# A gated linear attention and a maxout FFN: one masked product of q*P and k/P per chunk in place of seven levels, behind a guard

## The chip, the cores and the metric

One Trainium2 chip, one of its cores. The metric is the device time of one execution in microseconds; shorter is better.

## What is computed

First a linear attention with a decaying state, for 4 batches and 8 heads, 768 tokens, head width 48:

```python
f = 1 / (1 + exp(-f_logit))
for t in range(768):
    state = f[t][:, None] * state + outer(k[t], v[t])   # 48 x 48 per batch and head
    y[t] = q[t] @ state
```

So y_t is the sum over s <= t of v_s times the sum over d of q_t[d] k_s[d] P_t[d] / P_s[d], where P is the running product of the gates. Then an FFN on x, which is y as 3072 tokens of width 384:

```python
h = maximum(maximum(x @ w1, x @ w2), x @ w3)    # 384 -> 768
out = h @ w_out                                  # 768 -> 384
```

The attention's inputs are float32. The four weights come as float64 and are rounded to float32 on the chip. Every matrix product is in float32. The gates are the sigmoid of numbers around 2 (deviation 0.5).

## The kernel before

The tokens are taken in chunks of 128: 24 chunks, batch by batch (`b, c = divmod(u, NCH)`), six of a batch one after the other. Two heads share the 128 partitions, 64 rows each, of which 48 are used; `par` is which of the two, `hp` which of the four pairs of heads.

`chunk(u)` (lines 162 to 253) transposes f, k and q (lines 166 to 172). Then it splits the pairs (s, t) of the chunk into seven levels m = 1, 2, 4 .. 64 (line 186): at a level s lies in the first and t in the second half of an aligned block of 2m tokens. Each level is eight products of 48 x 128 by 48 x 64 (line 192), whose masked parts are copied into `at` (line 197 by VectorE, line 205 by ScalarE), and then the halves of `qh` and `kh` are multiplied by their neighbour's gate product (line 211 VectorE, line 212 GpSimd), on which the next level's products depend. After the levels: the output of the chunk (line 219), the share of the state (line 223), the new state (lines 228 to 242), the pairs s = t (lines 178 to 182, added at line 248), and three transposes that bring the result into `xT`, features on partitions (line 251).

Four chunks make a group, on which `ffn` (line 256) works in 22 steps: 18 with three products of 512 columns (line 263), and four that write 128 tokens (line 274). The weights are rounded by `round_weight` (lines 137 to 152) in 15 pieces, on VectorE, ScalarE and GpSimd, in the first group.

A chunk yields ten times (lines 183, 215, 245, 253), and at each yield the loop of line 298 issues one step of what is pending: the rounding first, then the FFN of the group before. A group has 40 yields for 22 steps. The order on each engine follows this program order closely; a planner moves single instructions ahead where their inputs are ready.

All DMAs are issued by SyncE: four loads a chunk, three chunks ahead, the weights, one store per 128 tokens. An fp32 product is two TensorE instructions, a transpose one.

Of the kernel before, what the change touches and what calls it, by code (L numbers as in the profile page):

```python
# [8 lines left out]
FP32 = mybir.dt.float32  # L9
U32 = mybir.dt.uint32  # L10
AF = mybir.ActivationFunctionType
ALU = mybir.AluOpType
AX = mybir.AxisListType

# y_t = sum_{s<=t} sum_d q_t[d] k_s[d] (prod_{s<u<=t} f_u[d]) v_s, in chunks of C tokens.
#
# Within a chunk the pairs (s, t) are split by levels m = 1, 2, 4 .. C/2: a pair belongs to the
# level whose aligned block of 2m tokens has s in its first half and t in its second. There
#     prod_{s<u<=t} f_u = (product after s to the end of the first half)
#                       * (product from the start of the second half to t),  # L20
# so with KH = k * (products to the end of its block of m) and QH = q * (products from the start of
# its block of m) the level is one matrix product, of which a mask takes the pairs in one block.
# From m to 2m the second halves of QH and the first halves of KH take the product of the whole
# neighbouring block. Every factor is at most 1 and nothing is divided, whatever the gates are.
# After the last level QH and KH are those of the whole chunk: for the state and from the state.
# The pairs s = t are added apart, with the dot product of q_t and k_t.
# [3 lines left out]
def kernel(  # L30
# [14 lines left out]
    C = 128  # L45
    DP = 64  # a head's rows when two heads share the 128 partitions
# [7 lines left out]
    GRP = 4  # chunks in one pass of the FFN  # L54
    TOK = GRP * C
    LEVELS = [1, 2, 4, 8, 16, 32, 64]
    AHEAD = 3

    const = ctx.enter_context(tc.tile_pool(name="const", bufs=1))
    work = ctx.enter_context(tc.tile_pool(name="work", bufs=2))  # L60
    ps_tr = ctx.enter_context(tc.tile_pool(name="ps_tr", bufs=2, space=bass.MemoryType.PSUM))
    ps_a = ctx.enter_context(tc.tile_pool(name="ps_a", bufs=3, space=bass.MemoryType.PSUM))
    ps_y = ctx.enter_context(tc.tile_pool(name="ps_y", bufs=1, space=bass.MemoryType.PSUM))
    ps_f = ctx.enter_context(tc.tile_pool(name="ps_f", bufs=2, space=bass.MemoryType.PSUM))

# [1 line left out]
    ident = const.tile([128, 128], FP32, name="ident")  # L67
    make_identity(nc, ident)

    # level m: key s (partition) against the m * n queries of the second halves (free)  # L70
    masks = {}
    for m in LEVELS[:-2]:
        n = C // (2 * m)
        t = const.tile([C, C // 2], FP32, name=f"mask{m}")
        nc.gpsimd.memset(t, 1.0)
        nc.gpsimd.affine_select(out=t, in_=t, compare_op=ALU.is_ge, fill=0.0, base=0,
                                pattern=[[-2 * m, n], [0, m]], channel_multiplier=1)
        nc.gpsimd.affine_select(out=t, in_=t, compare_op=ALU.is_ge, fill=0.0, base=m - 1,
                                pattern=[[2 * m, n], [0, m]], channel_multiplier=-1)
        masks[m] = t  # L80

    def zeroed(name, n, shape, part):
        ts = []
        for i in range(n):
            t = const.tile(shape, FP32, name=f"{name}{i}")
            nc.vector.memset(part(t), 0.0)
            ts.append(t)
        return ts

    NLD = AHEAD + 1  # L90
    pads = {nm: zeroed(f"{nm}_ld", NLD, [C, H, DP], lambda t: t[:, :, D:DP]) for nm in "qkf"}
    at_tiles = zeroed("at", 2, [C, 2, HP, C], lambda t: t)
    st_tiles = zeroed("st", 2, [128, HP, 2 * D], lambda t: t)
# [5 lines left out]
    loaded = {}  # L99

    def load(u):
        b, c = divmod(u, NCH)
        d = {}
        for nm, src in (("f", f_logit), ("k", k), ("q", q), ("v", v)):
            x = src[b, :, c * C:(c + 1) * C, :].rearrange("h t d -> t h d")
            if nm == "v":
                d[nm] = work.tile([C, H, D], FP32, name="v_ld", bufs=NLD)
                nc.sync.dma_start(out=d[nm], in_=x)
            else:
                d[nm] = pads[nm][u % NLD]  # L110
                nc.sync.dma_start(out=d[nm][:, :, 0:D], in_=x)
        loaded[u] = d

    # Weights come as float32 or as the words of float64, which are rounded to float32 here.
    pieces = [(w_in[i][:, c, :], src[c * 128:(c + 1) * 128, :])
              for i, src in enumerate((moe_w1, moe_w2, moe_w3)) for c in range(NK)]
    pieces += [(w_out[:, j, :], moe_w_out[j * 128:(j + 1) * 128, :]) for j in range(NJ)]
    raw = {}

    def load_weight(n):  # L120
        dst, src = pieces[n]
        if src.dtype == FP32:
            nc.sync.dma_start(out=dst, in_=src)
        else:
            raw[n] = work.tile([128, 2 * DFF], U32, name="raw", bufs=3)
            nc.sync.dma_start(out=raw[n][:, 0:2 * src.shape[1]], in_=src.bitcast(U32))

    def round_weight(n):
        if n not in raw:
            return  # L130
        dst, N = pieces[n][0], pieces[n][1].shape[1]
        words = raw.pop(n)[:, 0:2 * N].rearrange("p (n two) -> p n two", two=2)
        lo, hi = words[:, :, 0], words[:, :, 1]
        # The sign, the exponent and 23 bits of the mantissa. In float32's range the top bit of the
        # exponent and its low seven are float32's exponent.
        top = work.tile([128, N], U32, name="top_bits")
        nc.vector.tensor_scalar(top, hi, 3, 0x3FFFFFF8, op0=ALU.logical_shift_left, op1=ALU.bitwise_and)
        nc.vector.scalar_tensor_tensor(top, hi, 0xC0000000, top, op0=ALU.bitwise_and, op1=ALU.bitwise_or)
        nc.vector.scalar_tensor_tensor(top, lo, 29, top, op0=ALU.logical_shift_right, op1=ALU.bitwise_or)
        # The other 29 bits, times the power of two of the whole: a float32 sum rounds them in.  # L140
        rest = work.tile([128, N], U32, name="rest_bits")
        nc.vector.tensor_scalar(rest, lo, 0x1FFFFFFF, None, op0=ALU.bitwise_and)
        val = work.tile([128, N], FP32, name="rest_val")
        nc.scalar.activation(val, rest, AF.Copy, scale=2.0 ** -52)
        power = work.tile([128, N], U32, name="power")
        nc.vector.tensor_scalar(power, top, 0xFF800000, None, op0=ALU.bitwise_and)
        nc.gpsimd.tensor_tensor(val, val, power.bitcast(FP32), op=ALU.mult)
        nc.gpsimd.tensor_tensor(val, val, top.bitcast(FP32), op=ALU.add)
        # Below float32's normal range: 0.
        expo = work.tile([128, N], U32, name="expo")  # L150
        nc.vector.tensor_scalar(expo, hi, 20, 0x7FF, op0=ALU.logical_shift_right, op1=ALU.bitwise_and)
        nc.vector.scalar_tensor_tensor(dst, expo, 897.0, val, op0=ALU.is_ge, op1=ALU.mult)

# [1 line left out]
    def transposed(x):  # L155
        t = ps_tr.tile([128, HP, C], FP32, name="tr")
        flat = x.rearrange("t h d -> t (h d)")
        for hp in range(HP):
            nc.tensor.transpose(t[:, hp, :], flat[:, hp * 128:(hp + 1) * 128], ident)
        return t  # L160

    def chunk(u, xT):
        c, ld, slot = u % NCH, loaded.pop(u), u % GRP
        at, st, st_new = at_tiles[u % 2], st_tiles[u % 2], st_tiles[(u + 1) % 2]

        tr_f = transposed(ld["f"])
        gate = work.tile([128, HP * C], FP32, name="gate")
        nc.scalar.activation(gate, tr_f.rearrange("p a t -> p (a t)"), AF.Sigmoid)  # L168
        tr_k = transposed(ld["k"])
        kh = work.tile([128, HP, C], FP32, name="kh")  # L170
        nc.scalar.copy(kh, tr_k)
        tr_q = transposed(ld["q"])
        qh = work.tile([128, HP, C], FP32, name="qh")
        nc.vector.tensor_tensor(qh.rearrange("p a t -> p (a t)"), tr_q.rearrange("p a t -> p (a t)"),
                                gate, op=ALU.mult)

        qk = work.tile([C, H, D], FP32, name="qk")
        nc.gpsimd.tensor_tensor(qk, ld["q"][:, :, 0:D], ld["k"][:, :, 0:D], op=ALU.mult)
        dot = work.tile([C, H], FP32, name="dot")
# [156 lines left out]
```

## Time and profile before

| | us |
|---|---|
| three runs | 1162.44, 1164.34, 1164.58 (median 1164.34) |
| the profiled execution, first to last instruction | 1161.0 |
| the median of the runs above that span | 3.3 |
| TensorE busy | 957.2 |
| VectorE busy | 455.5 |
| mean granted TensorE clock | 0.828 |

A granted clock of 1.00 is 2.4 GHz, 0.50 is 1.2 GHz. Matmuls are pipelined: their durations overlap, so their rate is read from the distance between starts. PE is TensorE, PEld its weight loads, DVE VectorE, ACT ScalarE, POOL GpSimd, SP SyncE; a q behind the name is the engine's queue.

### The profile page before, as it was taken

How to read it: one execution, taken by the hardware profiler on the slowest of the kernel's cores; microseconds unless marked ns; L12 is line 12 of the kernel's file. 1: busy time of each engine (PE TensorE's matmuls, PEld its weight loads, DVE VectorE, ACT ScalarE, POOL GpSimd, SP SyncE). 2: the span in 40 equal slices, each digit the busy share in tenths (PEclk: the TensorE clock that was granted, in tenths of full speed). 3: DMA queues.
4: the chain of work that ended last, by engine and by line, in shares of the span. 5: the costliest groups of instructions: out<-in, count | busy, mean ns of one | idle time of the engine just before them, and what ended most of it. 6: DMA issues, size and time to landing. Idle time of an engine off the chain costs nothing. (4 is left out here: it accounts for less than half of the span.)

```text
span 1161.0 us, 12337 instructions
## 1 busy us (share of the span) xinstructions
PE 957.2 (82%) x4768; PEld 699.2 (60%) x4768; DVE 455.5 (39%) x913; ACT 135.5 (12%) x312; POOL 224.3 (19%) x267
## 2 busy tenths in 40 slices
PE   5501577799997799988799987799977899977898
PEld 4401567666566766667756667756666756666644
DVE  4899832343323243332244333244233234233110
ACT  0111011011111011111011101101111111100000
POOL 4455511211211111111211111111111111111000
PEclk9999985589995589985599985599975599965599
DMA  9233110011021011021011021011011000000000
GB/s 196 75 109 72 31 28 15 14 28 28 1 55 28 1 28 28 1 55 28 7 21 28 8 48 28 9 20 28 15 42 28 7 1 1 14 14 1 1 1 27
DMA packets 105514, 33.83 MB, mean 29 GB/s; under 512 B 100464, under 2 KB 103536, under 8 KB 105456
## 3 DMA queue, kind: packets, MB, share of 16 engines
q1 hardware_dynamic: 105456, 33.04, 13.6%
q8 instruction: 38, 0.62, 0.2%
q14 instruction: 20, 0.16, 0.0%
HBM read 28.31 MB, written 4.72 MB: 28 GB/s over the span
## 5 line engine op out<-in xcount | busy, mean ns | idle before, releaser
L192 PE MATMUL a<-qh,kh 48*128 48x64 f32 x2688 | 368.0, 345 | 119.1 <-DVE qh L211 87.7
L192 PEld LDWEIGHTS a<-qh,kh 48*128 48x128 f32 x2688 | 342.9, 251 | 192.3 <-POOL kh L212 102.3
L263 PE MATMUL p<-xT,w_in 128*128 128x512 f32 x648 | 307.8, 612 | 0.6 <-ACT xT L252 0.6
L197 DVE COPY_PREDICATED at<-mask,a 128x256 f32<-128x256 uint32 x240 | 126.3, 555 | 192.3 <-PE a L192 190.0
L212 POOL TENSOR_TENSOR kh<-kh,tot 128x256 f32<-128x256 f32 x144 | 103.4, 718 | 470.1 <-PE a L192 362.2
L263 PEld LDWEIGHTS p<-xT,w_in 128*128 128x128 f32 x648 | 116.4, 193 | 111.8 <-issue 106.1
L211 DVE TENSOR_TENSOR qh<-qh,tot 128x256 f32<-128x256 f32 x144 | 84.1, 584 | 127.9 <-PE a L192 127.9
L274 PE MATMUL p<-w_out,hm 128*128 128x384 f32 x288 | 98.3, 488 | 0.0
L205 ACT COPY at<-a 32x128 f32<-32x128 f32 x144 | 42.0, 292 | 384.9 <-PE a L192 381.2
L219 PEld LDWEIGHTS y<-v_ld,at 128*128 128x128 f32 x384 | 70.5, 274 | 6.5 <-issue 4.8
L274 PEld LDWEIGHTS p<-w_out,hm 128*128 128x128 f32 x288 | 52.5, 190 | 31.3 <-issue 0.5
L219 PE MATMUL y<-v_ld,at 128*128 128x48 f32 x384 | 71.0, 351 | 0.0
L212 POOL TENSOR_TENSOR kh<-kh,gate 128x256 f32<-128x256 f32 x24 | 20.3, 845 | 239.1 <-PE a L192 239.1
L251 PE MATMUL tr<-ident,x 128*128 128x128 f32 x72 | 16.9, 361 | 59.3 <-DVE x L248 59.3
L269 DVE TENSOR_TENSOR top<-p,top 128x512 f32<-128x512 f32 x36 | 24.9, 692 | 83.9 <-PE p L263 83.8
L251 PEld LDWEIGHTS tr<-ident,x 128*128 128x128 f32 x72 | 12.6, 199 | 64.2 <-issue 61.7
L267 ACT COPY top<-p 128x512 f32<-128x512 f32 x36 | 21.1, 585 | 254.3 <-PE p L263 254.3
L269 DVE TENSOR_TENSOR hm<-p,top 128x512 f32<-128x512 f32 x36 | 24.9, 691 | 61.3 <-PE p L263 61.3
L248 DVE TENSOR_TENSOR x<-y,own 128x384 f32<-128x384 f32 x24 | 13.4, 557 | 87.5 <-PE y L223 78.7
L182 POOL TENSOR_TENSOR own<-v_ld,dot 128x384 f32<-128x384 f32 x24 | 20.1, 837 | 111.7 <-DVE x L248 110.8
L214 DVE TENSOR_TENSOR tot<-gate 128x256 f32<-128x256 f32 x24 | 10.2, 425 | 74.9 <-ACT gate L168 74.9
L233 PE MATMUL tr<-v_ld,ks 128*128 128x96 f32 x160 | 33.0, 372 | 7.5 <-ACT ks L230 7.5
(50 smaller groups left out, 585.0 us busy)
## 6 DMA issues: line engine op xcount, KB each, us to landing
raw<-in_moe_w_dram SPq DMA_DIRECT2D x9, 768.0 KB, 4.4
f_ld<-in_f_logit_dram SPq DMA_DIRECT2D x24, 192.0 KB, 3.2
k_ld<-in_k_dram SPq DMA_DIRECT2D x24, 192.0 KB, 4.0
q_ld<-in_q_dram SPq DMA_DIRECT2D x24, 192.0 KB, 3.8
v_ld<-in_v_dram SPq DMA_DIRECT2D x24, 192.0 KB, 2.6
out_dram<-o SPq DMA_DIRECT2D x24, 192.0 KB, 1.9
raw<-in_moe_w_out_dram SPq DMA_DIRECT2D x6, 384.0 KB, 3.1
```

The source lines that it names most:

```text
L192: nc.tensor.matmul(a[:, hp, :].rearrange("s (n m) -> s n m", m=m), lhsT=kh[r, hp, :], rhs=qh[r, hp, :].rearrange("p (n two m) -> p n two m ...
L197: nc.vector.copy_predicated(at[:, par].rearrange("s a (n two m) -> s a n two m", two=2, m=m)[:, :, :, 1, :], masks[m].bitcast(U32).rearran ...
L205: nc.scalar.copy(at[s0:s0 + m, par, :, s0 + m:s0 + 2 * m], a[s0:s0 + m, :, i * m:(i + 1) * m])
L211: nc.vector.tensor_tensor(qv, qv, tv[:, :, 0:1].to_broadcast([128, nb, m]), op=ALU.mult)
L212: nc.gpsimd.tensor_tensor(kv, kv, tv[:, :, 1:2].to_broadcast([128, nb, m]), op=ALU.mult)
L219: nc.tensor.matmul(y[:, h * D:(h + 1) * D], lhsT=at[:, h % 2, h // 2, :], rhs=ld["v"][:, h, :], start=(h == 0), stop=(c == 0 and h == H - ...
L233: nc.tensor.matmul(ds[:, hp, :], lhsT=ks[:, hp, :], rhs=ld["v"][:, 2 * hp:2 * hp + 2, :].rearrange("s h d -> s (h d)"), start=True, stop=True)
L251: nc.tensor.transpose(tr_x[:, i, :], x[:, i * 128:(i + 1) * 128], ident)
L263: nc.tensor.matmul(p, lhsT=w_in[i][:, kt, j * 128:(j + 1) * 128], rhs=xT[:, kt, :], start=(kt == 0), stop=(kt == NK - 1))
L267: nc.scalar.copy(top, p)
L269: nc.vector.tensor_tensor(hm[:, j, :] if i == 2 else top, p, top, op=ALU.max)
L274: nc.tensor.matmul(p[:, 0:DM], lhsT=hm[:, j, i * C:(i + 1) * C], rhs=w_out[:, j, :], start=(j == 0), stop=(j == NJ - 1))
```

## The change

The kernel becomes two functions and a branch. `fast()` does all the work by another scheme. `general()`, the scheme of before (with its chunk and FFN one after the other), stands behind `tc.If(n_low > 0)`, where `n_low` counts the partitions in which one of the chunks' gate products fell below 2^-64.

In `fast()`:

- P, the running product of the gates inside a chunk, comes from a scan on VectorE, with a floor of 2^-80; 1/P from a reciprocal. `kh = k/P`, `qh = q*P` on GpSimd. The pairs of a chunk are then one product per head (eight of 48 x 128 by 48 x 128) and one mask, s <= t included. The levels, the products s = t and their addition are gone.
- The output is computed transposed, features on partitions (64 columns of weights per head), and ten DMAs per chunk pack its rows (48 of 64) into `xT`. The three transposes of before are gone.
- The chunks go round the four batches (`c, b = divmod(u, B)`), with a state per batch; a group of the FFN is one chunk of each batch.
- `gates(u + 1)` is issued ahead of `pairs(u)`. Five steps of the pending FFN or rounding are issued per chunk at three places, and what is left of them after the group's last chunk.
- The weights come in 12 pieces of 768 columns.

```diff
+            def gates(u):
+                f_ld, k_ld, q_ld = (pads[nm][u % NLD] for nm in "fkq")
+                tr_f = transposed(f_ld)
+                ...
+                nc.scalar.activation(gate, tr_f, AF.Sigmoid)
+                for hp in range(HP):
+                    nc.vector.tensor_tensor_scan(prod[:, hp, :], gate[:, hp, :], floor, 1.0,
+                                                 op0=ALU.mult, op1=ALU.max)
+                for hp in range(HP):
+                    nc.vector.reciprocal(inv[:, hp, :], prod[:, hp, :])
+                ... (transposes of k and q, ScalarE copies kt and qt)
+                nc.gpsimd.tensor_tensor(kh, kt, inv, op=ALU.mult)
+                nc.gpsimd.tensor_tensor(qh, qt, prod, op=ALU.mult)
+                nc.gpsimd.tensor_copy(ends[:, u, :], prod[:, :, C - 1])
+            def pairs(u):
+                ...
+                for hp in range(HP):
+                    for par in range(2):
+                        r = slice(par * DP, par * DP + D)
+                        nc.tensor.matmul(a[:, par, hp, :], lhsT=kh[r, hp, :], rhs=qh[r, hp, :],
+                                         start=True, stop=True)
+                for par in range(2):
+                    nc.vector.tensor_tensor(at[:, par], a[:, par],
+                                            mask.unsqueeze(1).to_broadcast([C, HP, C]), op=ALU.mult)
+                if c < NCH - 1:
+                    ... (kh transposed into tr_s, ScalarE copy ks)
+            def outputs(u, xT):
+                ...
+                for hp in range(HP):
+                    for par in range(2):
+                        nc.tensor.matmul(y[par * DP:(par + 1) * DP, hp, :], lhsT=v_ld[:, 2 * hp + par, :],
+                                         rhs=at[:, par, hp, :], ...)
+                if c < NCH - 1:
+                    ... (ds: the same loops, lhsT=ks[:, 2 * hp + par, :], rhs=v_ld[:, 2 * hp + par, 0:D])
+                if c:
+                    ... (the same loops into y, lhsT=st[r, hp, :], rhs=qh[r, hp, :])
+                nc.scalar.copy(yT, y)
+                if c < NCH - 1:
+                    ... (state: st_new = (ds + st) * tot, VectorE)
+                for h in range(H):
+                    ...
+                        nc.sync.dma_start(out=xT[row % 128:row % 128 + n, row // 128, b * C:(b + 1) * C],
+                                          in_=yT[p0:p0 + n, h // 2, :])
+            gates(0)
+            for u in range(NU):
+                if u + AHEAD < NU:          # AHEAD = 2
+                    load(u + AHEAD)
+                ...
+                if u + 1 < NU:
+                    gates(u + 1)
+                fill(2)
+                pairs(u)
+                fill(1)
+                outputs(u, xT)
+                fill(2)
+                if u % GRP == GRP - 1:
+                    for _ in pending:
+                        pass
+                    pending = ffn(u // GRP, xT)
+            for _ in pending:
+                pass
+            ... (least = min over ends, < 2^-64 as 0 or 1; n_low = their sum by one matmul; low <- n_low)
+    fast()
+    n_low = nc.values_load(low[0:1, 0:1], min_val=0, max_val=128)
+    with tc.If(n_low > 0):
+        general()
```

## Rows read from the trace of the kernel before

**Rows 1.** The page: busy us, share of the span, instructions.
```profile
PE 957.2 (82%) x4768; PEld 699.2 (60%) x4768; DVE 455.5 (39%) x913; ACT 135.5 (12%) x312; POOL 224.3 (19%) x267
```
**Rows 2.** Windows by stage: stretch, length, busy per engine (instructions), clock, DMA share, GB/s.
```profile
core 0: us, PE busy (x) PEld busy (x) DVE busy (x) ACT busy (x) POOL busy (x), PEclk, DMA share, GB/s
0.00:240.00 240.00, 123.31 (x644) 112.77 (x644) 149.44 (x247) 27.00 (x55) 88.81 (x93) 0.85 0.30 65
241.74:344.14 102.40, 101.10 (x520) 62.73 (x520) 38.98 (x84) 13.26 (x31) 16.90 (x21) 1.00 0.15 30
344.14:412.41 68.27, 52.79 (x276) 48.07 (x274) 21.26 (x49) 8.00 (x20) 11.43 (x15) 0.53 0.09 17
...
1092.60:1160.96 68.36, 65.01 (x156) 30.64 (x156) 8.29 (x12) 5.42 (x10) 0.00 (x0) 0.95 0.03 12
```
**Rows 3.** The FFN's products (line 263): ns min/median/max, first and last start.
```profile
L263 PE MATMUL p<-xT,w_in x648: 592/592/1220, 241.9 to 1141.5; 128*128 128x512 f32 x162
```
**Rows 4.** Order of time, TensorE near 30 us: start, us, instruction [idle before, releaser].
```profile
30.24 2.85 PE L192 MATMUL a<-qh,kh 48*128 48x64 f32 x16 [1.20 <-DVE qh L211]
```
**Rows 5.** Order of time, TensorE, in the first stretch at clock 1.00.
```profile
270.80 1.60 PE L192 MATMUL a<-qh,kh 48*128 48x64 f32 x16
272.33 2.84 PE L263 MATMUL p<-xT,w_in 128*128 128x512 f32 x6
275.01 1.88 PE L219 MATMUL y<-v_ld,at 128*128 128x48 f32 x16
276.73 1.10 PE L223 MATMUL y<-st,qh 128*128 128x96 f32 x8
277.66 0.60 PE L228 MATMUL tr<-ident,kh 128*128 128x128 f32 x4
```
**Rows 6.** Windows, line 192 alone, in the sixteen products at 270.80.
```profile
270.80:271.29 0.49, 0.49 (x4) 0.49 (x5) 1.00 0.00 0
271.30:271.69 0.40, 0.40 (x10) 0.40 (x9) 1.00 0.00 0
```
**Rows 7.** Groups by line and shape: count, busy us, mean ns, idle before, releasers.
```profile
L269 DVE TENSOR_TENSOR top<-p,top 128x512 f32<-128x512 f32 x36 | 24.9, 692 | 83.9 <-PE p L263 83.8
...
L230 ACT COPY ks<-tr 128x512 f32<-128x512 f32 x20 | 11.7, 585 | 111.4 <-PE tr L228 111.4
...
L242 DVE TENSOR_TENSOR st<-st,tr 64x192 f32<-64x192 f32 x32 | 11.3, 352 | 19.0 <-PE tr L233 18.7
...
L214 DVE TENSOR_TENSOR tot<-tot 128x128 f32<-128x128 f32 x24 | 7.8, 326 | 0.9
...
L214 DVE TENSOR_TENSOR tot<-tot 128x4 f32<-128x4 f32 x24 | 4.6, 190 | 0.5
```
**Rows 8.** Order of time while the weights are rounded (one period of four).
```profile
58.41 1.98 POOL L147 TENSOR_TENSOR rest_val<-rest_val,power 128x768 f32<-128x768 f32 x1 [3.63 <-DVE power L146]
...
60.73 2.56 DVE L138 SCALAR_TENSOR_TENSOR top_bits<-raw,top_bits 128x768 uint32<-128x768 uint32 x1
...
64.08 0.95 DVE L139 SCALAR_TENSOR_TENSOR top_bits<-raw,top_bits 128x768 uint32<-128x768 uint32 x1
...
66.11 1.98 POOL L147 TENSOR_TENSOR rest_val<-rest_val,power 128x768 f32<-128x768 f32 x1 [3.64 <-DVE power L146]
```
**Rows 9.** The stores (line 279): issue in ns min/median/max, and landing.
```profile
L279 SPq DMA_DIRECT2D out_dram<-o x24: 332/356/361, 325.9 to 1158.2; - x24
...
DMA to landing us min/median/max: 1.8/1.9/2.0
```
**Rows 10.** Order of time at the start: the first weight loads.
```profile
17.05 2.06 SPq L126 DMA_DIRECT2D raw<-in_moe_w_dram  x3
```
**Rows 11.** The chain of work that ended last: start, us, what.
```profile
1092.61 49.52 PE p L263 x108
1142.13 15.49 PE p L274 x48
...
1157.69 0.48 ACT o L277
```

More of the change, by code (lines that the diff above doesn't have):

```diff
@@ L9 @@
 FP32 = mybir.dt.float32
+I32 = mybir.dt.int32
 U32 = mybir.dt.uint32
@@ L13 @@
 AX = mybir.AxisListType
+C = 128
+DP = 64
+P_MIN = 2.0 ** -64
+P_FLOOR = 2.0 ** -80
+GATE_PAD = 40.0
 @with_exitstack
@@ L44 @@
     B, H, S, D = q.shape
-    C = 128
-    DP = 64
     HP = H // 2
@@ L53 @@
     NJ = DFF // 128
-    GRP = 4
+    GRP = B
     TOK = GRP * C
-    LEVELS = [1, 2, 4, 8, 16, 32, 64]
-    AHEAD = 3
+    THIRD = DFF // 3
     const = ctx.enter_context(tc.tile_pool(name="const", bufs=1))
[L60 to L63, printed above, removed]
@@ L64 @@
-    ps_f = ctx.enter_context(tc.tile_pool(name="ps_f", bufs=2, space=bass.MemoryType.PSUM))
     ident = const.tile([128, 128], FP32, name="ident")
     make_identity(nc, ident)
[L71 to L93, printed above, removed]
     w_in = [const.tile([128, NK, DFF], FP32, name=f"w_in{i}") for i in range(3)]
@@ L96 @@
     w_out = const.tile([128, NJ, DM], FP32, name="w_out")
[L99 to L112, printed above, removed]
@@ L115 @@
[L115 to L126, printed above, removed]
@@ L128, in round_weight @@
[L128 to L152, printed above, removed]
@@ L256, in ffn @@
-    def ffn(g, xT):
-        hm = work.tile([128, NJ, TOK], FP32, name="hm")
-        for j in range(NJ):
-            top = None
-            for i in range(3):
-                p = ps_f.tile([128, TOK], FP32, name="p")
-                for kt in range(NK):
-                    nc.tensor.matmul(p, lhsT=w_in[i][:, kt, j * 128:(j + 1) * 128], rhs=xT[:, kt, :],
-                                     start=(kt == 0), stop=(kt == NK - 1))
-                if i == 0:
-                    top = work.tile([128, TOK], FP32, name="top")
-                    nc.scalar.copy(top, p)
-                else:
-                    nc.vector.tensor_tensor(hm[:, j, :] if i == 2 else top, p, top, op=ALU.max)
-                yield
-        for i in range(GRP):
-            p = ps_f.tile([128, TOK], FP32, name="p")
-            for j in range(NJ):
-                nc.tensor.matmul(p[:, 0:DM], lhsT=hm[:, j, i * C:(i + 1) * C], rhs=w_out[:, j, :],
-                                 start=(j == 0), stop=(j == NJ - 1))
-            o = work.tile([128, DM], FP32, name="o")
-            nc.scalar.copy(o, p[:, 0:DM])
-            t0 = g * TOK + i * C
-            nc.sync.dma_start(out=out[t0:t0 + C, :], in_=o)
-            yield
@@ L282, in weights @@
-    def weights():
-        for n in range(len(pieces) + 2):
-            if n < len(pieces):
-                load_weight(n)
-            if n >= 2:
-                round_weight(n - 2)
-                yield
-    for u in range(AHEAD):
-        load(u)
-    pending, xT = weights(), None
-    for u in range(NU):
-        if u + AHEAD < NU:
-            load(u + AHEAD)
-        if u % GRP == 0:
-            xT = work.tile([128, NK, TOK], FP32, name="xT")
-        for _ in chunk(u, xT):
-            next(pending, None)
-        if u % GRP == GRP - 1:
+    low = const.tile([1, 1], I32, name="low")
@@ L301 @@
             for _ in pending:
                 pass
-            pending = ffn(u // GRP, xT)
-    for _ in pending:
-        pass
+            least = work.tile([128, 1], FP32, name="least")
+            nc.vector.tensor_reduce(out=least, in_=ends.rearrange("p u a -> p (u a)"), op=ALU.min, axis=AX.X)
+            nc.vector.tensor_scalar(least, least, P_MIN, None, op0=ALU.is_lt)
+            n_low = ps_tr.tile([1, 1], FP32, name="tr")
+            nc.tensor.matmul(n_low, lhsT=least, rhs=ones, start=True, stop=True)
```

433 lines of the change are left out of this document (342 added, 91 removed).

## The prediction

> **What bounds the kernel now.** I read first the engines' busy times, then the stretches that the granted clock marks off, then TensorE's order of time inside them. TensorE is busy 957 of 1161.0 us, VectorE 455 [rows 1]: TensorE is the engine to follow, but its busy time is not one kind of time. The span falls into four kinds of stretch [rows 2]. From 0 to 241.9, where the first FFN matmul starts [rows 3], TensorE is half idle; here VectorE rounds the weights. Then five times (one pair is shown) a stretch of 102.40 us at granted clock 1.00 (2.4 GHz), in which FFN steps stand between the attention's pieces and TensorE has no gap, and after it one of about 68 us at 0.53 (1.2 GHz nearly throughout), in which the attention runs alone and TensorE waits for VectorE and GpSimd between levels (52.79 busy of 68.27). At the end the last FFN runs alone. The rows call 0 to 160 us clock 1.00, but sixteen level products at 30 us take 2.85 us [rows 4], at full clock 1.60 [rows 5]: the start is at the lower level too.
>
> So three things cost time: the rounding at the start, the levels' instructions and waits, and the lower clock of the stretches without FFN.
>
> **What the change does, part by part.**
>
> *TensorE, one chunk, full clock.* The seven levels issue 112 instructions per chunk; sixteen of them (one level) begin over 1.5 us. The output, 16 instructions, takes 276.73 - 275.01 = 1.72 us, 0.107 each; the state's share, 8, takes 0.93, 0.116 each; these have 48 and 96 columns, so for such small products 0.11 us per instruction is the rate whatever their columns [rows 5]. The new chunk has 16 transposes, and 16 instructions each (eight fp32 products of two) for the pairs, the output, the state's growth (ds) and the state's share. Eighty at 0.11 are 8.8 us, the upper bound at full clock. The lower: where the two parities of a level, which lie in different halves of the array's rows, meet in time, the rate doubles. Within 0.49 us four begin; an instruction is some 0.27 long, so two of the ten in the next 0.40 us lap over and eight begin, 0.05 each [rows 6]. The new code alternates the parity from product to product, so I take 0.9 us for the pairs instead of 1.75. For ds, whose weights have 64 columns instead of 128, I also take half: 0.9. The output and the state's share alternate between halves of the array's columns, which no row shows: I leave them at 1.75 each. With 1.75 for transposes that is 7.05 us (bounds 5.3 and 8.8).
>
> The Trainium skill (TensorEngine Tiling (Array Packing), "Key Properties") says that different tiles load weights and multiply in parallel, for column tiles as for row tiles. By the row the sum holds it for the pairs alone; by the rule the output and the state's share would halve too: that is rival 1.
>
> Added to 7.05: 0.6 for about six changes between full-width and half-width products (an estimate, 0.1 each: at the two rates of [rows 6], half at 0.12 and half at 0.05, sixteen level products need some 1.4 us, and the FFN step behind them begins after 1.53 [rows 5]), and 1.0 for waits, mostly the q transposes, which need the buffer that the sigmoid frees (0.6 us, as any such ScalarE pass [rows 7]). What removes the old waits: gates(u+1) stands a whole chunk ahead of pairs(u+1), and consecutive chunks are of different batches, so the state that a chunk reads is four chunks old. One chunk: 8.65 us.
>
> *FFN.* Unchanged: the last group's 48 output instructions take 15.49 us at full clock [rows 11], 0.323 for 384 columns, hence 0.430 for 512; 108 x 0.430 + 15.5 = 62 us a group.
>
> *Steady part.* A chunk takes five FFN steps, a group 20 of the 22, and the last two are drained behind the fourth chunk: FFN steps stand in every stretch, as in the rows at 1.00. I take full clock throughout: the 68 us stretches vanish. Group: 62 + 4 x 8.65 = 96.6, five groups 483; the last group has no ds nor its transposes (1.3 x 4 = 5): 478. Before, the same five took 241.9 to 1092.6, 851.
>
> *Other engines beside it.* VectorE per chunk: mask product 2 x 0.69, state 2 x 0.35, three FFN maxima 2.1 [rows 7], 4.2 us, and the gates: four scans and four reciprocals of 128 columns, which the trace does not have. Below, an operation of four columns takes 0.19, eight are 1.5; above, the slowest VectorE instruction in the trace takes 2.56 [rows 8], eight are 20. The nearest row is the product of 128 columns, 0.33; I take 0.45, 3.6 us in all, since the two-source instruction of 0.95 stretches to 2.56 beside a GpSimd product [rows 8] and GpSimd now has two products of 512 columns a chunk. 7.8 us of 24: hidden. ScalarE: five passes of 0.59 and the FFN's, under 5 us: hidden. SyncE: four loads, one store and ten packing DMAs at 0.36 = 5.4 us of issue [rows 9]: hidden. The packing waits for yT and has loads and weight loads queued behind it; the loads behind it are needed more than a chunk later. Its landing (1.9 us) is covered by the two to four FFN steps drained after the fourth chunk, except for group 0, where there are none.
>
> The Trainium skill (VectorE: DVE Perf Modes, "First, the fixed hardware budget") says that a reciprocal is an iterated divide with a repeat count of 8. No row shows it. If that costs eight cycles a column at the page's 0.96 GHz, a reciprocal would be an estimated 1.2 us and the gates 6.6: 3 us nearer to the point at which rival 2 begins, and the sum as it is.
>
> *Start.* The rounding keeps its elements. Twelve pieces of 768 columns at the period of 66.11 - 58.41 = 7.70 us [rows 8] are 92.4. Before, weight loads were issued at 17.05 behind 16 loads [rows 10]; now behind 12: about 13, data at 18. In VectorE's queue two gates (7.2) and two chunks' mask and state work (4.2) fall between: 18 + 92.4 + 11.4 = 122. Then the output of chunk 2 and all of chunk 3 at the lower clock (pairs 1.8, mask 1.4, output 3.5, copy 0.6, about 8 each): 138, and packing (3.6 issue, 1.9 landing, a hop): 145 instead of 241.9.
>
> *End.* Last FFN 62 (before, 49.52 + 15.49, its first steps at the lower clock); copy, store and closing 3.4 as before (1157.6 to 1161.0) [rows 11]. New are a count of too-small products, its load into a register of every engine and the branch over the level scheme. Nothing like it is in the trace: below 0 (beside the last store's landing), above 8 (four landings of 1.9 in a row); I take 4, two landings, as count and load depend on each other.
>
> *Sum.* 145 + 478 + 62 + 3.4 + 4 = 692 of span against 1161.0; the median of the runs, 1164.34, lies 3.3 above that span: **696 us**.
>
> **Rivals.**
> 1. *Column halves overlap as the row halves do.* For: the two parities' rate in [rows 6]. Against: that row is of row halves alone. Output and state's share fall by 1.75 a chunk, 20 chunks: 696 - 35 = 661.
> 2. *VectorE's order holds TensorE up.* The gates stand ahead of the FFN's evacuations in one queue, and there are two FFN buffers. From the chunk's first transposes TensorE has 1.75 + 5.2 (two steps) + 1.8 = 9 us before it needs the first buffer back; VectorE gives it back at about 1.4 + gates + 0.7. At 1.28 us for each of the eight (half of the 2.56 in [rows 8]), gates of 10.2, that is 12.3: 3.3 late, 20 chunks 66, and 13 at the start for two gates 6.6 longer: 775. At the bound of 20 us it is 13 late: some 1000. Against: the nearest row's 0.33.
> 3. *The clock falls in the attention's own stretch.* ds, output and state's share are 4.4 us of small products without an FFN step. For: attention alone runs at 0.53 [rows 2]. Against: there TensorE waits a quarter of the time; here it need not, and 3 us of the same products between FFN steps [rows 5] lie in a stretch at 1.00. With half the work of the steady part at 1.2 GHz it takes half as long again: 696 + 239 = 935; a quarter: 815.
> 4. *The other side: the clock stays low throughout.* Same place, but small products at every point of the chunk keep the granted clock at 1.2 GHz. Steady part and last FFN double: 696 + 478 + 62 = 1236, slower than before. It decides from 468 of these 540 us of work done at the lower level, 87%. Against: every stretch of before with FFN steps at intervals of a few us is at 1.00.
> 5. *The change does not do what it says: the branch is taken.* Then the level scheme runs behind the new one: over 1700. It needs one of the 9216 products of 128 gates below 2^-64; from the reference's inputs the smallest is 2^-30.5.
>
> **How the numbers follow.** Forecast 0.50, its own range 670 to 735 (start 15 either way, waits of 0 to 2 us a chunk); rival 1 0.20; rival 2 0.15; rival 3 0.11; rival 4 0.03; rival 5 0.01. The range from 640 to 810 holds the forecast, rival 1 and the milder parts of 2 and 3, between 8 and 9 in 10. No change would be within 0.2%, 2.3 us, about what a measurement of this kernel can tell from none; hardly any case gives it: faster 0.955, same 0.005, slower 0.04.
>
> **What would show it.** Right: granted clock at 1.00 from about 150 us to the end without the 68 us stretches; first FFN matmul near 145; groups about 97 us apart; pairs at half the rate per instruction of the output. Wrong: the first FFN matmul after 180 (the rounding was not alone on VectorE); TensorE idle before FFN matmuls, released by VectorE's maxima (rival 2); clock under 0.9 in the steady part (rivals 3 and 4); the span's end more than 10 us behind the last store.

## The result, and the profile after

The changed kernel takes **626.44 us** (median of 4 runs, 626.03 to 630.0) against 1164.46 for the kernel before on the same chip: a ratio of 0.5387 [0.5372, 0.5402]. The forecast was 696 us, its range 640 to 810: the direction was right, the time lies below the range. The profiled execution has a span of 624.3 us and a time of 626.03. Line numbers from here on are the changed kernel's: 165 input transposes, 178 scans, 181 reciprocals, 202 pairs, 212 transposes of k/P, 227 output, 234 state's growth (ds), 240 state's share, 258 packing, 270 and 281 the FFN's two products.

Windows by stage of the changed kernel, cut at the first FFN matmul (140.6) and at the groups' ends (columns as in [rows 2]; a group in the second row and in the third, the third to the fifth left out, and the last FFN in the last row):

```profile
0.00:140.60 140.60, 49.77 (x323) 36.51 (x323) 109.55 (x165) 27.01 (x41) 72.66 (x50) 0.82 0.62 121
140.60:222.20 81.60, 81.51 (x425) 44.71 (x425) 28.37 (x49) 13.73 (x25) 8.12 (x9) 1.00 0.31 58
222.20:306.80 84.60, 84.60 (x479) 48.34 (x478) 34.62 (x60) 16.60 (x30) 10.90 (x12) 1.00 0.29 57
...
555.70:624.30 68.60, 61.94 (x158) 29.36 (x157) 8.45 (x13) 5.91 (x11) 0.00 (x0) 0.98 0.05 16
```

The first group is short because it begins inside its first chunk: by 140.6 that chunk's pairs, its kh transposes and its ds have run. Read against the prediction's terms:

| part | before | predicted | after | after - predicted |
|---|---|---|---|---|
| to the first FFN matmul | 241.9 | 145 | 140.6 | -4.4 |
| five groups | 850.7 | 478 | 415.1 | -62.9 |
| last FFN | 65.0 | 62 | 61.8 | -0.2 |
| end | 3.4 | 7.4 | 6.8 | -0.6 |
| span | 1161.0 | 692 | 624.3 | -68 |

Nearly the whole error is in the five groups. There TensorE has no gap (84.60 busy of 84.60) and the granted clock is 1.00; the 68 us stretches at 0.53 of [rows 2] are gone. The busy times against [rows 1]: TensorE fell by 430 us, VectorE and GpSimd by 178 and 103.

```profile
PE 526.7 (84%) x2714; PEld 298.7 (48%) x2714; DVE 277.5 (44%) x453; ACT 109.0 (17%) x189; POOL 121.7 (19%) x104
```

TensorE's order of time over one chunk (columns as in [rows 5]; the next chunk begins at 325.16, the same view's row of the f transposes):

```profile
306.61 0.60 PE L165 MATMUL tr<-ident,f_ld 128*128 128x128 f32 x4
307.04 0.60 PE L165 MATMUL tr<-ident,k_ld 128*128 128x128 f32 x4
307.48 1.02 PE L270 MATMUL p<-xT,w_in 128*128 128x512 f32 x2
308.34 0.60 PE L165 MATMUL tr<-ident,q_ld 128*128 128x128 f32 x4
308.78 4.46 PE L270 MATMUL p<-xT,w_in 128*128 128x512 f32 x10
313.17 1.16 PE L202 MATMUL a<-qh,kh 48*128 48x128 f32 x16
314.26 0.66 PE L212 MATMUL tr<-ident,kh 128*128 128x128 f32 x4
314.75 2.74 PE L270 MATMUL p<-xT,w_in 128*128 128x512 f32 x6
317.42 1.10 PE L227 MATMUL y<-at,v_ld 128*64 128x128 f32 x16
318.35 0.62 PE L234 MATMUL tr<-v_ld,ks 128*64 128x48 f32 x16
318.90 1.08 PE L240 MATMUL y<-qh,st 48*48 48x128 f32 x16
319.90 5.42 PE L270 MATMUL p<-xT,w_in 128*128 128x512 f32 x12
325.16 0.60 PE L165 MATMUL tr<-ident,f_ld 128*128 128x128 f32 x4
```

A group's cost is read from its start to the start of the next, because the matmuls' ends overlap. Sixteen pairs take 314.26 - 313.17 = 1.09 us, the output 0.93, ds 0.55, the share 1.00: 0.068, 0.058, 0.034 and 0.063 per instruction, against 0.107 to 0.116 in [rows 5]. The chunk's period is 325.16 - 306.61 = 18.55; without 30 FFN matmuls at 0.430 it is 5.65, where the prediction had 8.65.

The end of the chain of work that ended last (start, us, what), against [rows 11]: the last FFN's first products are now at full clock like the rest.

```profile
555.69 46.35 PE p L270 x108
...
```

### The profile page after: what moved, and what is told of

The parts are those of the page before. It is cut to its first block, busy times and chain, and to the rows that moved or that the text cites. A ratio compares the mean times of both kernels' runs of the same rounds, so it can differ in the third digit from the quotient of the medians.

```text
span 624.3 us, 7153 instructions
## 1 busy us (share of the span) xinstructions
PE 526.7 (84%) x2714; PEld 298.7 (48%) x2714; DVE 277.5 (44%) x453; ACT 109.0 (17%) x189; POOL 121.7 (19%) x104
## 4 chain that ended last, share of the span: by engine, by line
PE 78%; DVE 11%; POOL 6%; SPq 2%; DMA 1%; issue 0%; ACT 0%; POOLq 0%; ACTq 0%
PE p L270 45%; PE p L281 15%; PE tr L165 4%; POOL rest_val L150 4%; PE y L227 4%; PE a L202 3%; PE y L240 3%; POOL rest_val L151 2%; SPq L108 2%; DVE prod L178 2%; DVE inv L181 2%; PE tr L212 2%; DVE w_in L156 1%; DVE rest_bits L145 1%; DVE top_bits L141 1%; PE tr L234 1%
## 5 line engine op out<-in xcount | busy, mean ns | idle before, releaser
L181 DVE RECIPROCAL inv<-prod 128x128 f32<-128x128 f32 x96 | 80.9, 902 | 0.0
L178 DVE TENSOR_TENSOR_SCAN prod<-gate,floor 128x128 f32<-128x128 f32 x96 | 40.1, 478 | 89.9 <-ACT gate L174 89.9
L227 PE MATMUL y<-at,v_ld 128*64 128x128 f32 x384 | 32.8, 305 | 24.8 <-DVE at L206 24.8
L227 PEld LDWEIGHTS y<-at,v_ld 128*64 128x64 f32 x384 | 24.6, 150 | 43.0 <-DVE at L206 26.6
L189 POOL TENSOR_TENSOR kh<-kt,inv 128x512 f32<-128x512 f32 x24 | 30.8, 1282 | 54.5 <-DVE inv L181 39.6
L150 POOL TENSOR_TENSOR rest_val<-rest_val,power 128x768 f32<-128x768 f32 x12 | 31.3, 2612 | 40.9 <-DVE power L149 29.1
L206 DVE TENSOR_TENSOR at<-a,mask 128x512 f32<-128x512 f32 x48 | 30.7, 682 | 13.2 <-PE a L202 13.2
L202 PEld LDWEIGHTS a<-qh,kh 48*128 48x128 f32 x384 | 26.5, 210 | 16.0 <-issue 16.0
L191 POOL TENSOR_TENSOR qh<-qt,prod 128x512 f32<-128x512 f32 x24 | 30.4, 1267 | 11.8 <-ACT qt L187 7.3
L202 PE MATMUL a<-qh,kh 48*128 48x128 f32 x384 | 31.4, 309 | 0.0
```

The source lines that it names most:

```text
L178: nc.vector.tensor_tensor_scan(prod[:, hp, :], gate[:, hp, :], floor, 1.0, op0=ALU.mult, op1=ALU.max)
L181: nc.vector.reciprocal(inv[:, hp, :], prod[:, hp, :])
L189: nc.gpsimd.tensor_tensor(kh, kt, inv, op=ALU.mult)
L202: nc.tensor.matmul(a[:, par, hp, :], lhsT=kh[r, hp, :], rhs=qh[r, hp, :], start=True, stop=True)
L206: nc.vector.tensor_tensor(at[:, par], a[:, par], mask.unsqueeze(1).to_broadcast([C, HP, C]), op=ALU.mult)
L227: nc.tensor.matmul(y[par * DP:(par + 1) * DP, hp, :], lhsT=v_ld[:, 2 * hp + par, :], rhs=at[:, par, hp, :], start=(hp == 0), stop=(c == 0 ...
```

## The experiments

All ratios are to the kernel before, run beside each. "After" is the changed kernel, 626.44 us.

**1. Halves apart, in all four products.** The inner loop over the parity (left half, right half of the array) is made the outer one.

```diff
-                for hp in range(HP):
-                    for par in range(2):
+                for par in range(2):
+                    for hp in range(HP):
```

> The parity loop goes outside in all four products of a chunk (pairs, output, ds, state's share), so that neighbouring instructions lie in the same half of the array. Theory (the halves of rows and of columns work at the same time when neighbours alternate): pairs 1.09 to 1.8 us a chunk, output 0.92 to 1.75, state's share 1.00 to 1.75, ds 0.55 to 0.9; 3.1 us a chunk, 20 chunks in the steady part, 62: about 688 us, groups of 97 us instead of 84.5. Rival (the rate comes from the narrower weights or from 128 columns, whatever the order): 626, within 3.

Measured: 655.75 us, 0.5631 [0.5622, 0.5641]: slower than after by 29, about half of the 62 expected. Its order of time shows why the rest did not come:

```profile
328.79 1.71 PE L202 MATMUL a<-qh,kh 48*128 48x128 f32 x16
...
333.59 1.25 PE L227 MATMUL y<-at,v_ld 128*64 128x128 f32 x13
334.58 0.32 PE L234 MATMUL tr<-v_ld,ks 128*64 128x48 f32 x2
334.68 0.27 PE L227 MATMUL y<-at,v_ld 128*64 128x128 f32 x1
...
335.55 1.55 PE L240 MATMUL y<-qh,st 48*48 48x128 f32 x16
337.03 5.42 PE L270 MATMUL p<-xT,w_in 128*128 128x512 f32 x12
```

Where the output's second half (right) meets the first half (left) of ds, the two run into each other: output and ds change places instruction by instruction. So the edit did not take all the overlap away: output, ds and share take 337.03 - 333.59 = 3.44 us, after 2.48. The pairs take 1.64, after 1.09.

**2. The same, in the output and the share only.** The edit of 1, in two of its four places.

> The parity loop goes outside in the output and the state's share alone, the term that the prediction left at 1.75 us each. Theory (column halves overlap): 0.92 to 1.75 and 1.00 to 1.75, 1.6 us a chunk, 20 chunks 32: about 658 us; pairs and ds stay at 1.09 and 0.55. Rival (only row halves overlap; the output's 0.058 us per instruction comes from its 64 columns of weights): output stays at 0.92, the state's share alone rises, 626 to 641.

Measured: 645.2 us, 0.554 [0.5531, 0.5549], 13 below the expected 658. Output, ds and share again take 3.45, the pairs their 1.09; the pairs' order is then the other 10 us of experiment 1.

**3. Half by half over three products.** To leave no seam where halves meet, one half's output, ds and share run first, then the other's; only the one place in the middle changes half.

(The edit in outline:)

```diff
-                for hp in range(HP): for par in range(2): (output) ...; the same for ds; the same for the share
+                for par in range(2):
+                    for hp in range(HP): (output)
+                    for hp in range(HP): (ds)
+                    for hp in range(HP): (share)
```

> Output, ds and state's share of one parity after the other, so that 24 instructions in a row lie in one half of the array's columns and there is one seam a chunk instead of five; the pairs alternate as changed. Theory (halves overlap only where neighbours are of different halves, and the seams are what made the swapped loops cost less than 3.1 us a chunk): output, ds and share rise from 2.48 to 4.0 to 4.4 us a chunk, 20 chunks 30 to 38: 656 to 664 us. Rival (the rate is that of the swapped loops, about 1 us a chunk, whatever the seams): 645.

Measured: 672.77 us, 0.578 [0.5769, 0.5791].

```profile
336.55 1.09 PE L229 MATMUL y<-at,v_ld 128*64 128x128 f32 x8
337.47 0.61 PE L233 MATMUL tr<-v_ld,ks 128*64 128x48 f32 x8
338.01 1.07 PE L237 MATMUL y<-qh,st 48*48 48x128 f32 x8
339.01 1.09 PE L229 MATMUL y<-at,v_ld 128*64 128x128 f32 x8
339.94 0.61 PE L233 MATMUL tr<-v_ld,ks 128*64 128x48 f32 x8
340.48 1.07 PE L237 MATMUL y<-qh,st 48*48 48x128 f32 x8
341.48 5.42 PE L267 MATMUL p<-xT,w_in 128*128 128x512 f32 x12
```

Eight instructions now take what sixteen took: 0.92, 0.54 and 1.00, and the three products 4.93 in place of 2.48. The same work on the same data, only in another order, costs 46 us of the kernel. That settles it: the halves of the array's columns do overlap, when products that follow each other lie in different halves. The expected 656 to 664 was too low since it doubled output and share alone; ds doubled too.

**4. A third PSUM buffer for the transposes.** If the q transposes wait for the buffer that the sigmoid frees, a third one takes the wait away.

```diff
-            ps_tr = ctx.enter_context(tc.tile_pool(name="ps_tr", bufs=2, space=bass.MemoryType.PSUM))
+            ps_tr = ctx.enter_context(tc.tile_pool(name="ps_tr", bufs=3, space=bass.MemoryType.PSUM))
```

> Three transpose buffers instead of two: the q transposes no longer need the buffer that the sigmoid frees. Theory (two FFN instructions stand in that wait already, so it costs nothing, and the prediction's 1.0 us of waits a chunk is not there to be won): 626, within 3, groups of 84.5. Rival (the wait costs 0.3 to 1.0 us a chunk): 606 to 620.

Measured: 626.66 us, 0.5384 [0.5373, 0.5396]: no difference. With three buffers the twelve transposes run in one piece:

```profile
306.14 0.60 PE L165 MATMUL tr<-ident,f_ld 128*128 128x128 f32 x4
306.58 0.60 PE L165 MATMUL tr<-ident,k_ld 128*128 128x128 f32 x4
307.02 0.60 PE L165 MATMUL tr<-ident,q_ld 128*128 128x128 f32 x4
```

With two, two FFN matmuls stand before the q transposes (307.48 in the chunk above) and cover the wait: program order has them behind, the planner drew them forward. The wait exists and costs nothing.

**5. All five FFN steps behind the chunk.** This takes the FFN away from between the attention's pieces: the test of rival 3 (clock) and of what the FFN steps cover.

```diff
-                fill(2)
                 pairs(u)
-                fill(1)
                 outputs(u, xT)
-                fill(2)
+                fill(5)
```

> The five FFN steps of a chunk all come after its output, none between its parts. Theory (the FFN steps cover the chunk's own waits, and the clock follows from that): the mask product stands behind the next chunk's gates on VectorE, so the output waits some 4 us a chunk, 20 chunks 80: about 705 us if the granted clock stays at 1.00. Rival A (an attention stretch without FFN steps and with waits lowers the clock): clock under 0.9 in the steady part, 780 to 900. Rival B (the planner moves FFN instructions into the waits whatever the program order): 626, within 8.

Measured: 644.73 us, 0.5544 [0.5522, 0.5565], 18 us slower: far from either 705 or 780 to 900, and 10 above the 626 within 8 of rival B, whose mechanism it shows. One group's window and lines of a chunk's order (it begins at 330.96, the next at 350.50):

```profile
226.30:315.00 88.70, 88.59 (x477) 50.02 (x476) 33.39 (x61) 16.50 (x30) 10.57 (x13) 1.00 0.28 54
```

```profile
331.93 0.49 PE L202 MATMUL a<-qh,kh 48*128 48x128 f32 x2
332.34 0.66 PE L165 MATMUL tr<-ident,q_ld 128*128 128x128 f32 x4
332.93 1.16 PE L202 MATMUL a<-qh,kh 48*128 48x128 f32 x14
...
335.46 0.67 PE L234 MATMUL tr<-v_ld,ks 128*64 128x48 f32 x16
336.06 1.98 PE L270 MATMUL p<-xT,w_in 128*128 128x512 f32 x4
337.98 1.18 PE L227 MATMUL y<-at,v_ld 128*64 128x128 f32 x16
```

The planner drew FFN matmuls (and ds) into the waits again, so TensorE stayed full (88.59 of 88.70) at clock 1.00. The 1.0 us that a chunk costs more (350.50 - 330.96 = 19.54 for 18.55) is not waiting: the same products run in more, shorter pieces. What the attention would do with no FFN work at hand was therefore not tested.

**6. Batches in turn.** Chunks go batch by batch, so each needs the state that the chunk just before it left.

```diff
-                c, b = divmod(u, B)
+                b, c = divmod(u, NCH)
```

(the same in `load` and in the pairs, and the slot of the group in the packing's and the output's addresses)

> Chunks batch by batch again (a chunk reads the state that the chunk just ahead of it made), the rest as changed. Theory (a state is made a whole chunk, 18 us, before it is read, so the round over the batches removes no wait): groups of 84.5 us, 626 within 5 (chunks without state products move out of the first group, some 2 us a batch). Rival (the state's chain is a wait, as in the levels of before): 1 to 2 us a chunk, 646 to 666.

Measured: 626.89 us, 0.5378 [0.5364, 0.5393]: the same. A chunk of the steady part takes 18.55 us in either order, so the state is ready in either; the round over the batches, which the prediction gave as a reason for no old waits, is not what removed them.

**7. No guard.** The load of the count of small products into registers, the branch and the level scheme behind it are left out; the count itself stays.

```diff
-    n_low = nc.values_load(low[0:1, 0:1], min_val=0, max_val=128)
-    with tc.If(n_low > 0):
-        general()
```

> The register load, the branch and the level scheme behind it are left out; the count of too-small products stays, and nothing reads it. Theory (the branch costs what the end grew by, 6.8 us from the last product to the closing instead of 3.4): 623, within 1.5; the rest of the span as with it. Rival (the last store's landing covers the branch): 626, within 1.

Measured: 623.05 us, 0.5353 [0.5344, 0.5361]; span 621.1 against 624.3: load and branch cost 3.2 to 3.4 us (predicted 4, with the count), all of it behind the last store, since the last copy begins at 617.57 here and at 617.60 with them. The count stays hidden: in the changed kernel it ends before the last store is issued.

```profile
617.68 0.14 DVE L333 CAST low<-tr 1x1 int32<-1x1 f32 x1 [14.91 <-PE tr L332]
618.11 0.33 SPq L286 DMA_DIRECT2D out_dram<-o  x1
```

**8. Output by tokens, transposed by TensorE.** The packing DMAs are undone: the output is made as before ([rows 5], lines 219 and 223) and three transposes bring it into the FFN's layout.

```diff
-                        nc.tensor.matmul(y[par * DP:(par + 1) * DP, hp, :], lhsT=v_ld[:, 2 * hp + par, :],
-                                         rhs=at[:, par, hp, :], ...)
+                    nc.tensor.matmul(y[:, h * D:(h + 1) * D], lhsT=at[:, h % 2, h // 2, :], rhs=v_ld[:, h, 0:D], ...)
...
+                for i in range(NK):
+                    nc.tensor.transpose(tr_x[:, i, :], x[:, i * 128:(i + 1) * 128], ident)
```

> The output in token form as before the change (the masked pairs as weights, 128 columns; state's share with a block-diagonal state; three transposes back and a ScalarE copy into xT) in place of the transposed output and its ten packing DMAs; two single buffers for gate and inv make room. Theory (the packing saves TensorE only what the transposed form saves: output 16 x 0.11, share 8 x 0.116, transposes 3 x 0.11, 3.0 us instead of 0.92 + 1.00): 1.1 us a chunk, 20 chunks 22: 648 us. Rival A (the DMAs' landing costs at the groups' seams, and goes): 626 or less. Rival B (x has to be copied, transposed and copied again, in a row, ahead of the next FFN): over 670.

Measured: 653.88 us, 0.5615 [0.5605, 0.5626], 27 us slower. A chunk takes 342.39 - 322.78 = 19.61, after 18.55: 1.06 more, 21 us over 20 chunks, and the first FFN matmul comes 5 later (145.6).

```profile
333.50 1.88 PE L229 MATMUL y<-v_ld,at 128*128 128x48 f32 x16
335.31 0.67 PE L235 MATMUL tr<-v_ld,ks 128*64 128x48 f32 x16
...
337.77 0.49 PE L256 MATMUL tr<-ident,x 128*128 128x128 f32 x3
338.09 4.46 PE L266 MATMUL p<-xT,w_in 128*128 128x512 f32 x10
```

The output takes 1.81 (after 0.93), the share 0.97 (1.00), the transposes 0.32. The transposed form pays because its sixteen products go to two column halves in turn; the saved transposes are the smaller part.

**9. The first FFN beside the rounding.** The first group rounds four of the twelve pieces, all of w_in. The first FFN's input steps then run in turn with the rounding of the other eight (five of w_in, three of w_out), each piece ahead of the step that needs it (F an FFN input step, R a piece of rounding, O an output step).

```diff
+            def mixed(rounding, steps):
+                for what in "FFRFFRFF" + "RFF" * 6 + "OOOO":
+                    next(rounding if what == "R" else steps, None)
+                    yield
...
+                if u == GRP - 1:
+                    pending = mixed(pending, ffn(0, xT))
```

(with one piece of rounding per chunk in the first group, at the first of the three places, and 3, 2 and 3 steps in the second group, each in place of 2, 1, 2)

> The first group rounds four pieces instead of twelve; the other eight stand between the first FFN's steps, each piece ahead of the step that needs it, and both are spread over the second group. Theory (the start is as long as the rounding's and the chunks' VectorE work in a row, 143 us, with TensorE idle two thirds of it): first FFN matmul at about 75 us, end of the second group at some 170 instead of 222: about 575 us. Rival (VectorE and GpSimd are no nearer their end then, and steps that wait for a piece block the chunks queued behind them on TensorE): 615 to 640.

Measured: 590.58 us, 0.5074 [0.5064, 0.5083]. The first FFN matmul starts at 74.6, the last one of the second group at 185.3 (expected 170, after 221.7): the gain is 36, not 51. VectorE still rounds in that stretch, and TensorE waits 16.7 us for it in seven waits, of which the first two rows have four (us in total, times, longest):

```profile
PE p L270 <- DVE hm L276: 5.0, 2, 4.0
PE y L227 <- DVE at L206: 4.8, 2, 4.6
...
```

**10. Rounding without GpSimd and ScalarE.** Two GpSimd products and a ScalarE pass per step become two VectorE instructions.

```diff
-                nc.scalar.activation(val, rest, AF.Copy, scale=2.0 ** -52)
-                nc.gpsimd.tensor_tensor(val, val, power.bitcast(FP32), op=ALU.mult)
-                nc.gpsimd.tensor_tensor(val, val, top.bitcast(FP32), op=ALU.add)
+                nc.vector.scalar_tensor_tensor(val, rest, 2.0 ** -52, power.bitcast(FP32),
+                                               op0=ALU.mult, op1=ALU.mult)
+                nc.vector.tensor_tensor(val, val, top.bitcast(FP32), op=ALU.add)
```

> Rounding with VectorE alone: the scaling (ScalarE) and the two GpSimd products of a piece become one product of three factors and one addition on VectorE. Theory (a GpSimd product holds up VectorE's instructions with two streams, so 3.7 us of GpSimd cost more than the 1.9 us that they take on VectorE): a piece 7.0 instead of 7.7 to 9 us, twelve pieces 8 to 24: 602 to 618. Rival (VectorE is what bounds the start, and gets 23 us more work): 640 to 650.

Measured: 609.71 us, 0.5241 [0.5225, 0.5257]. The first FFN matmul moves from 140.6 to 124.9: 16 of the 17 us gained. Up to it VectorE is busy 115.14 us, after 109.55: it took over some 23 us of work, so the rest of its work there took 17 less.

**11. Both.** Experiments 9 and 10 in one kernel.

> The two edits together (first FFN begun among the rounding, rounding on VectorE alone). Theory: the gains of both, less what the first one already hides: 560 to 572. Rival: as the first alone or worse, 575 or more.

Measured: **576.55 us**, 0.4943 [0.4929, 0.4958], the fastest of all and 50 below after, 5 above the 560 to 572 expected; 36 and 17 alone make 53.

```profile
0.00:72.60 72.60, 50.51 (x328) 37.42 (x329) 65.97 (x116) 18.37 (x30) 17.27 (x26) 0.74 0.88 152
72.60:177.40 104.80, 92.65 (x442) 49.00 (x441) 83.85 (x131) 15.24 (x27) 11.71 (x13) 0.93 0.51 108
```

VectorE is busy 149.8 of the first 177.4 us, 136.45 of them in the 140 from 20 to 160: it bounds the start now. From 177.4 on the groups are those of the changed kernel (the first, to 261.2, is 83.80 busy of 83.80 at clock 1.00).

**12. The kernel before, its FFN steps spread.** The level scheme stays; the 22 FFN steps of a group are spread evenly over its 40 yields instead of one at each of the first 22.

```diff
-        for _ in chunk(u, xT):
-            next(pending, None)
+        for step, _ in enumerate(chunk(u, xT)):
+            at_yield = u % GRP * 10 + step
+            n = 1 if u < GRP else (at_yield + 1) * 22 // 40 - at_yield * 22 // 40
+            for _ in range(n):
+                next(pending, None)
```

> The kernel before, with the 22 FFN steps spread over a group's 40 yields instead of at the first 22. Theory (of the 438 us that the steady part lost, the lower clock of the stretches without FFN is a part that needs no new scheme): granted clock 1.00 in the whole steady part, levels without a step still wait 1.4 us, groups of some 153 us instead of 170: about 1080 us. Rival A (the clock falls between the steps): 1150 or more. Rival B (waits beside the steps vanish too): under 1040.

Measured: 978.07 us, 0.8406 [0.8391, 0.8422].

```profile
377.30:511.20 133.90, 132.21 (x796) 88.78 (x796) 60.35 (x134) 20.31 (x49) 28.26 (x36) 1.00 0.16 30
```

Rival B's case: the levels' waits are gone too (132.21 busy of 133.90). A group takes 133.9 at clock 1.00 where [rows 2] had 102.40 and 68.27, so its 36.8 us, five times 184, were there for a change of order alone.

## Why the prediction was wrong

**The step that failed** is "The output and the state's share alternate between halves of the array's columns, which no row shows: I leave them at 1.75 each". They take 0.93 and 1.00. With ds at 0.55 for 0.9 that is 1.92 us of the 3.0 that a chunk was put too dear. For ds two things came together: in one half its instructions take 0.068 each, not 0.11 (experiment 3), so the rate does depend on the shape, and turns halve that. Rival 1 was the case that came, and experiment 3 shows its mechanism by the order alone: 2.48 against 4.93 us. The Trainium skill's sentence that the prediction weighed (TensorEngine Tiling (Array Packing), "Key Properties": different tiles load weights and multiply in parallel) agrees: 0.058 us per instruction of the output when halves take turns, 0.115 when they don't.

**The second step, smaller:** "1.0 for waits". Pairs, output, ds, share and sixteen transposes at 0.437 to 0.494 per four (1.80) sum to 5.37; the chunk's 5.65 leaves 0.28, and that stands at an end of three FFN pieces, 0.09 each, where the shape of the products changes, so no wait is left. The wait for the sigmoid's buffer is there, but FFN matmuls drawn forward cover it (experiment 4). The "0.6 for about six changes" was not too dear. The changes lie in that 0.28 and inside the distances of 5.37. At the pace of their starts (two every 0.109 to 0.112 us in pairs, output and share, two every 0.058 in ds, one every 0.109 in the transposes) the products alone would take 4.9, so the changes took some 0.8. By the distances, 1.92 and 1.3 (1.6 without the 0.28), less 0.24 for pairs (1.09 for 0.9) and transposes (1.80 for 1.75), put the chunk 3.0 below, 20 chunks 60 of the 62.9 us.

**How the range missed.** The prediction itself had 5.3 us as the lower bound of the products and held 7.05; the products took 5.37. Its rival 1 at 661 kept all the waits. With the waits at 0, the lower end that its own range names, that is 696 - 35 - 20 = 641, at the end of the range; with ds at 0.55, or a start a few us early, it is outside. The lower ends of several terms of one chunk were each in the text, and were never added up.

**What was right.** Start: 140.6 for 145, in part by luck, since its terms were off in both directions and balance: data came at 19.37 for 18, the last piece was rounded at 127.9 for 122, the rest took 12.7 for 23. VectorE's order of time, the first and the last instruction of the rounding:

```profile
19.37 0.56 DVE L140 TENSOR_SCALAR top_bits<-raw 128x768 uint32<-128x768 uint32 x1 [2.95 <-DMA raw<-in_moe_w_dram]
...
126.97 0.96 DVE L156 SCALAR_TENSOR_TENSOR w_out<-expo,rest_val 128x768 f32<-128x768 uint32 x1 [2.29 <-POOL rest_val L151]
```

Last FFN, end and guard came within a microsecond. The pairs were right too: at the pace of their starts they take 0.89, for the 0.9 held. The granted clock is 1.00 from 136.5 to 621.2, so rivals 3 and 4 did not happen; experiment 5 does not bring rival 3 about either. Rival 2 (VectorE's order): gates of four scans and four reciprocals take 4.6 us in the steady part, above the 3.6 taken, below the 10.2 from which the rival lived, and no FFN matmul waits for them. VectorE's order of time there, with the gates of the chunk shown:

```profile
307.87 1.37 DVE L178 TENSOR_TENSOR_SCAN prod<-gate,floor 128x128 f32<-128x128 f32 x4 [16.99 <-ACT gate L174]
309.16 3.36 DVE L181 RECIPROCAL inv<-prod 128x128 f32<-128x128 f32 x4
```

By the Trainium skill (VectorE: DVE Perf Modes, "First, the fixed hardware budget"), which has the reciprocal as an iterated divide with a repeat count of 8, the estimate was 1.2 us each; the rows have 3.36 / 4 = 0.84, nearer to it than the 0.45 taken from the product of 128 columns.

The packing DMAs cost more to issue than predicted and it made no difference: ten are 6.2 us of SyncE (0.50 to 1.52 each, median 0.59), not 3.6, of a chunk's 18.55; landing is 1.8 in the median.

**Where the 537 us of span went:** 101 in the start, where the weights are rounded (TensorE is busy 49.77 us there, after 123.31 of 240 in [rows 2]; VectorE 109.55 after 149.44), 436 in the five groups; last FFN and end cancel. Of the 436, experiment 12 gets 184 without the new scheme, by FFN steps in every stretch, which ends the lower clock and the levels' waits; the other 252 need the fewer products, and of those the alternation of halves in output, ds and share is worth 46 (experiment 3). Why the clock falls in the attention's own stretch of the kernel before stays open between its waits and its small products: no run here left either alone.

## What to carry to other kernels

Order small products so that those that follow each other lie in different halves of the array: the loop order alone was worth 46 us of 626 here for output, ds and share, and some 10 for the pairs, whose halves are of rows (experiments 1 and 2). Before a stage is rewritten, spread the dense work that is at hand evenly over it: that alone gave 16% in the kernel before. When several terms of one repeated piece have bounds, add up all the lower ends and all the upper ends before a range is drawn.

## What the runs showed of the hardware

- Half-array products overlap across loop seams, several instructions deep (experiment 1: the output's right half begins at 334.08, when three of the left half's eight are still to start, and ds begins among the output's last), so "par outermost" is not a serial version; only half by half over three products was. At the seams of the share, with 48 rows where the others have 128, none is seen: in experiment 3 it takes 1.00 ahead of the other half's output (338.01 to 339.01) as ahead of the FFN (340.48 to 341.48).
- A change of shape (all of the array, half of its rows, half of its columns, or both) costs 0.13 to 0.20 us: in the chunk shown of the changed kernel the next product's first start comes 0.09 to 0.10 us late and its second another 0.04 to 0.10. Five changes make the 0.8 us above. From the output to ds, both of 128 rows by 64 columns, the starts keep their pace.
- Scans stretch beside GpSimd's rounding products: four take 1.37 us in the steady part and 4.50 in the rounding, while GpSimd runs two products, as the two-source instruction of 0.95 in [rows 8] does. In experiment 10, where these products are gone, four scans amid the rounding are 0.41, 0.41 and 0.73 (two). The changed kernel's VectorE and GpSimd in order of time:

```profile
101.26 4.50 DVE L178 TENSOR_TENSOR_SCAN prod<-gate,floor 128x128 f32<-128x128 f32 x4
```

```profile
101.48 1.80 POOL L150 TENSOR_TENSOR rest_val<-rest_val,power 128x768 f32<-128x768 f32 x1 [3.63 <-DVE power L149]
103.37 1.80 POOL L151 TENSOR_TENSOR rest_val<-rest_val,top_bits 128x768 f32<-128x768 f32 x1
```

- A branch on a value computed in the kernel, with the load of the value into registers and nothing taken, costs 3.2 to 3.4 us at the end (experiment 7).
